# Moving four output stores behind a query transpose, and reordering batch 0's mean products

## The chip, the cores and the metric

The kernel runs on one core of one Trainium2 chip. The metric is the device time of one execution in microseconds (us). TensorE is called PE, VectorE DVE, ScalarE ACT, GpSimd POOL; SyncE (SP) issues transfers only. A row with a q (SPq, POOLq) is the issue of a transfer on that engine's queue.

## What is computed

Linear attention over 8 batches, 8 heads, 576 positions and 64 channels per head, followed by a feed-forward block over the 512 channels of all heads:

```
q_s = exp(q) / sum over channels        k_s = exp(k) / sum over positions
kv  = k_s^T v   (per head, 64 x 64)     x   = q_s kv   (576 x 512 per batch)
xn  = (x - mean(x)) / sqrt(var(x) + 1e-6) * g
out = x + relu(xn @ w1) @ w2            w1: 512 x 2048, w2: 2048 x 512
```

The maxima that the reference takes off before the exponentials cancel in the quotients. Inputs and output are float32; the products run in bfloat16.

## The kernel before

The 576 positions of a batch are cut into 512 main positions (4 tiles t of 128) and 64 left over. A chunk c from 0 to 7 is the main part of batch c; chunk 8 gathers the left-over positions of all batches. For each chunk the feed-forward products are a list of small steps, `mlp_steps(c)`. Beside it stands a list of side steps with hand-written positions, which prepare the next batches: loads, exponentials, transposes, kv products and x. `run(main, side)` merges the two lists by position, so the order on every engine is the one written by hand (`manual_schedule`); each engine takes its instructions strictly in that order and waits on semaphores where data is missing.

**What lies around the stores.** Chunk 0's outputs come from `y_out` (L512): DVE forms `ot` (L516), and POOL's queue stores it (L522), 256 KB each, four in all, one for each tile t. They come at the end of chunk 0's steps. Then `run` for c = 1 begins, with the side steps of `second_side` (L889): batch 2's queries are exponentiated (positions 3 and 9) and transposed by a transfer on SP's queue (`eq_T(2)`, position 14, L253). At 14.1 `load_batch(3, (2,), ...)` lets POOL copy four elements of the transposed queries eqT into batch 3's query buffer (L1114, a CAST in the profile), so that SP's load of batch 3's queries (L117) starts only when the transposes have landed. At 14.2 `load_v(3)` has POOL load batch 3's v (vt, vr; L144, L147). Behind SP's loads of q, k and the rest of k (ktr, L124) stand, on the same queue, the transposes of chunk 2's normalised x (`xn_T`, xnT). From xnT, POOL forms the differences tq (`sum_x`, L245) that chunk 2's first layer uses: `mm1_fast` (L751) computes it as products of sums and differences of blocks, with banks bx, bb and bc. The buffers `ot` are a ring of four; chunk 1's outputs (`y_quarter`, L607) write the same four again.

**What lies around the mean.** Batch 0 is the start of the kernel. There x is built transposed: `xt_mm(j)` multiplies the queries of tiles 0 and 1 with kv for block j of 128 channels. The mean over channels is a product as well: `mean0(i)` scales a constant matrix by a row sum of kv (DVE, L320), and `mean_mm(i, ns)` adds the i-th of four such products to target n: 0 is the mean alone (xm), 1 and 2 are blocks 2 and 3 of x. Blocks 0 and 1 get the mean added later on DVE (`xt_out(0)`, `xt_out(1)`, L356); blocks 2 and 3 have it in the bank already (L361 on DVE, L363 on ACT). Behind these PE has eight po products for x itself, then the transposes of query tile 2 (`eq_pT(0, 2)`, L932), which need ACT's exponential of the second half of batch 0's q.

Of the kernel before, what the change touches and what calls it, by code (L numbers as in the profile page):

```python
# [20 lines left out]
def kernel(  # L21
# [16 lines left out]
    nc = tc.nc  # L38

    B, H, S, D = q.shape  # L40
# [3 lines left out]
    T = 4  # L44
    SM = P * T
# [3 lines left out]
    NP = H // 2  # L49
# [51 lines left out]
    def main_src(x, b, h0, hn):  # L101
        return x[b, h0 : h0 + hn, 0:SM, :].rearrange("h (p t) d -> p h (t d)", t=T)
# [19 lines left out]
    def load_krem(eng, b):  # L122
        for half in range(2):
            eng.dma_start(  # L124
                raws[b][3][SR * half : SR * half + SR],
                k[b, 4 * half : 4 * half + 4, SM:S, :].transpose([1, 0, 2]),
            )
# [11 lines left out]
    def load_v(b):  # L139

        vts[b] = mlp.tile([P, H, T, D], BF16, tag="vt", name="vt", bufs=1)
        if b == 1:
            load_krem(nc.gpsimd, b)
        nc.gpsimd.dma_start(vts[b].rearrange("p h t d -> p h (t d)"), main_src(v, b, 0, H))  # L144
        for half in range(2):
            hs = slice(4 * half, 4 * half + 4)
            nc.gpsimd.dma_start(  # L147
                vr[SR * half : SR * half + SR, b % 2, hs, 0:D],
                v[b, hs, SM:S, :].transpose([1, 0, 2]),
            )  # L150
# [13 lines left out]
    eks, eqs, eqTs, xs, xnTs, rstds, tqs = {}, {}, {}, {}, {}, {}, {}  # L164
# [21 lines left out]
    def exp_q(b, j, hn=2):  # L186
        if j == 0:
            new_eq(b)
        hs = slice(2 * j, 2 * j + hn)
        nc.scalar.activation(  # L190
            eqs[b][0][:, :, hs, :].rearrange("p t h d -> p h t d"),
            raws[b][2][:, hs], AF.Exp,
        )
# [11 lines left out]
    def reduce_q(c, t, tn=1):  # L205
        ts = slice(t, t + tn)
        nc.vector.reduce_sum(eqs[c][1][:, ts], eqs[c][0][:, ts], axis=AX.X)  # L207
# [49 lines left out]
    def eq_T(c):  # L257
        dma_T(eqTs[c], eqs[c][0].rearrange("p t h d -> p (t h d)"), 0, T)
# [63 lines left out]
        )  # L322

    def mean_mm(i, ns):
        if i == 0 and 0 in ns:
            kvbox["m"] = mm_ps.tile([P, 2, 2, P], FP32, tag="m", name="xm")[:, 0]
            both = mm_ps.tile([P, 2, 2, P], FP32, tag="m", name="xt")
            kvbox["xt", 2], kvbox["xt", 3] = both[:, 0], both[:, 1]
        for n in ns:
            nc.tensor.matmul(  # L330
                (kvbox["m"], kvbox["xt", 2], kvbox["xt", 3])[n], mean_w[:, i],
                eqTs[0][:, 0:2, i, :], start=(i == 0 and n < 2), stop=(i == NP - 1),
                skip_group_check=True,
            )

    def xt_mm(j):

        if j < 2:
            kvbox["xt", j] = att_ps.tile([P, 2, 2, P], FP32, tag="a", name="xt")[:, 0]
        nc.tensor.matmul(  # L340
            kvbox["xt", j], kv_sb[:, 0, j, :], eqTs[0][:, 0:2, j, :],
            start=(j < 2), stop=(j < 2), skip_group_check=True,
        )

    def y_mul(j):
# [81 lines left out]
    def square_sum(c, t):  # L427
        x, _, _, mv = xs[c]
        nc.scalar.activation(  # L429
            scrap, x[:, t], AF.Square, bias=mv[:, t, 0:1], scale=-float(DM),  # L430
            accum_out=mv[:, t, 1:2],
        )
# [26 lines left out]
    def rstd_op(c):  # L459
        mv = xs[c][3]  # L460
        lnv = sml.tile([P, T], FP32, tag="lnv", name="lnv")
        rstds[c] = mlp.tile([P, T], FP32, tag="rstd", name="rstd")
        nc.scalar.activation(
            lnv, mv[:, :, 1], AF.Ln, bias=eps_ln, scale=1.0 / DM ** 3
        )
        nc.scalar.activation(rstds[c], lnv, AF.Exp, scale=-0.5)
# [24 lines left out]
    def mm1_part(c, m, t0, tn, ko):  # L491
# [13 lines left out]
        if m % 2 == 1 and at + tn == 2 and ko == KO1 - 1:  # L505
# [3 lines left out]
            else:  # L509
                nc.scalar.activation(dst, ph, AF.Relu)  # L510

    def y_out(c, t, pc, cols=slice(0, 512), eng=None):  # L512
        if cols.start == 0:
            hbox["ot"] = outp.tile([P, DM], FP32, tag="ot", name="ot")
        ot = hbox["ot"][:, cols]
        nc.vector.scalar_tensor_tensor(  # L516
            ot, in0=pc, scalar=rstds[c][:, t : t + 1], in1=xs[c][0][:, t, cols],
            op0=ALU.mult, op1=ALU.add,
        )
        eng = eng or nc.gpsimd  # L520
        if c < B:
            eng.dma_start(  # L522
                out[c, 0:SM, :].rearrange("(p t) n -> p t n", t=T)[:, t, cols], ot
            )
        else:
            for half in range(2):
                eng.dma_start(
                    out[2 * t + half, SM:S, cols], ot[64 * half : 64 * half + 64]
                )

    def mm2(c, t, ko):
        if ko == 0:
            hbox["pc"] = mm_ps.tile([P, DM], FP32, tag="m", name="pc")
        nc.tensor.matmul(
            hbox["pc"], hbox["h"][:, ko, t, :], w2_sb[:, ko, :],
            start=(ko == 0), stop=(ko == KO2 - 1),
        )
        if ko == KO2 - 1:
            y_out(c, t, hbox["pc"])
# [12 lines left out]
    def quarter_w2(i, g):  # L552

        ks = slice(4 * g, 4 * g + 4)
        rows = [w2_sb[:, 8 * g + odd : 8 * g + 8 : 2, :] for odd in range(2)]
        (b11, b12), (b21, b22) = [(r[:, :, 0:DH2], r[:, :, DH2:DM]) for r in rows]
        t1, t2, t3, t4 = [w2_q[:, n, ks, :] for n in range(4)]
        dst, x, y = ((t1, b12, b11), (t3, b22, b12), (t2, b22, t1), (t4, b21, t2))[i]
        nc.vector.tensor_sub(out=dst, in0=x, in1=y)
# [329 lines left out]
    def second_side():  # L889

        s = [(p, lambda i=i: quarter_w2(i, 1)) for i, p in enumerate((13, 16, 44, 46))]
        s += [(8, lambda: xn_pT(1, 2, nc.scalar)), (12, lambda: xn_pT(1, 3, nc.vector))]
        s += [(3, lambda: exp_q(2, 0, 4)), (9, lambda: exp_q(2, 2, 4)), (14, lambda: eq_T(2))]
        s += [(42, lambda: square_sum(1, 2)), (67, lambda: square_sum(1, 3)), (71, lambda: rstd_op(1))]
        s += [(14.1, lambda: load_batch(3, (2,), eqTs[2][0:1, T - 1, NP - 1, 0:4])), (31, lambda: load_batch(3, (0,)))]
        s += [(18 + 2 * j, lambda j=j: cast_v(2, j)) for j in range(2)]
        s += [(14.2, lambda: load_v(3))]
        s += [(93 + j, lambda j=j: cast_v(3, j)) for j in range(2)]
        s += [(15 + 3 * t, lambda t=t: reduce_q(2, t, 2)) for t in (0, 2)]
        s += [(36, lambda: recip_q(2))]  # L900
        s += [(18, lambda: exp_k(2, 0, 4)), (22, lambda: exp_k(2, 2, 4)), (26, lambda: prep_kvrem(2))]
        s += [(41, lambda: kv_all(2))]
        s += [(46, lambda: start_x(2))]
        for t, (p0, p1) in enumerate(((52, 54), (57, 59), (62, 65), (70, 74))):
            s += spread([lambda t=t, i=i: po_mm(2, t, i) for i in range(NP)], p0, p1)
            s += [(p1, lambda t=t: x_fast(2, t)), ((73, 82, 88, 94)[t], lambda t=t: square_sum(2, t))]
        s += [(60, lambda: xn_T(2, 0, 2)), (77, lambda: xn_T(2, 2, 2)), (100, lambda: rstd_op(2))]
        s += [(75, lambda: exp_q(3, 0, 4)), (79, lambda: exp_q(3, 2, 4)), (85, lambda: eq_T(3))]
        s += [(97, lambda: exp_k(3, 0, 4)), (108, lambda: exp_k(3, 2, 4)), (113, lambda: prep_kvrem(3))]
        s += [(p, lambda i=i: sum_w1(i, 1)) for i, p in ((2, 28), (3, 30))]  # L910
        s += spread([lambda i=i: sum_x(2, i) for i in range(4)], 95, 108)
        return s
# [39 lines left out]
    def xn_pT(c, t, eng):  # L952
        pe_T(xnTs[c], xs[c][2][:, t], t, eng, None if c else g_col)
# [7 lines left out]
    def first_batch():  # L961
# [94 lines left out]
        y_mul(0)  # L1056
        xt_mm(1)
        y_mul(1)
        for i in range(2):
            mean_mm(i, (0,))  # L1060
        for i in range(2):
            mean_mm(i, (1, 2))
        xt_mm(2)
        xt_mm(3)
        for i in (2, 3):
            mean_mm(i, (0,))
        for i in (2, 3):
            mean_mm(i, (1, 2))
        exp_qt(0, 2)
        exp_qt(0, 3)  # L1070
        xt_out(0)
# [1 line left out]
        for t in range(2):  # L1073
            pobox[0, t] = mm_ps.tile([P, DM], FP32, tag="m", name="po")
            for i in range(NP):
                nc.tensor.matmul(
                    pobox[0, t][:, i * P : i * P + P], eqTs[0][:, t, i, :], kv_sb[:, 0, i, :],
                    start=True, stop=True,
# [28 lines left out]
    def load_batch(b, parts=(2, 0), after=None):  # L1107

        alloc(b, parts)
        for which in parts:  # L1110
            if after is None:
                nc.vector.memset(raws[b][which][0:1, 0, 0, 0:1], 0.0)
            else:
                nc.gpsimd.tensor_copy(out=raws[b][which][0:1, 0, 0, 0:4], in_=after)  # L1114
        for which in parts:
            load_main(nc.sync, b, which, 0, H)
        if 0 in parts:
            load_krem(nc.sync, b)
# [102 lines left out]
```

## Time and profile before

| | |
|---|---|
| median of 3 runs | 265.62 us (264.61 to 266.18) |
| profiled execution | 265.17 us, of which the span of the profile is 263.0 us |
| granted clock of PE | 0.996 of full speed, mean |
| DMA | 45.00 MB, mean 171 GB/s |
| stores of the output on POOL's queue | 32 of 256 KB, median 5.9 us from issue to landing |
| transposes of the queries on SP's queue | 7, median 4.9 us from issue to landing |

How to read the lines shown: in a group or timeline row stand the start and the busy time in us (in the page's groups only the busy time), the engine, the line of the kernel, the operation, output and input, the shape, the count, and in square brackets how long the engine sat idle before it and what ended that. A row of the chain is start, duration and work; "DMA" in it is a transfer from issue to landing. A row of the table of windows gives, for each engine, its busy time in that stretch with the count of instructions, then the granted clock, the share of the 16 DMA engines' time that was busy, and GB/s.

### The profile page before, as it was taken

Reading aid. Unit: us, or ns where it says so; the run is one execution under the profiler, and the core shown is the slowest. Engines: PE = TensorE matmul, PEld = TensorE weight load, DVE = VectorE, ACT = ScalarE, POOL = GpSimd, SP = SyncE. Lnnn points to the kernel's source line nnn. Section 1 sums busy time; section 2 is a strip of 40 time slices with the busy share of each in tenths; the row PEclk is TensorE's granted clock in tenths of the full one; section 3 lists DMA queues with packets and bytes.
Section 4 is the critical chain, followed back from the end, with each engine's and each line's share of the span. In section 5 each row is a group of like instructions: output and inputs, shape, how many; then the busy total and the mean of one; then the engine's idle time right before and its main releaser. Section 6 shows DMA issues by size and latency. Waiting matters only on the chain.

```text
span 263.0 us, 6841 instructions
## 1 busy us (share of the span) xinstructions
PE 255.7 (97%) x2708; PEld 216.9 (82%) x2711; DVE 217.6 (83%) x482; ACT 180.5 (69%) x357; POOL 77.8 (30%) x129
## 2 busy tenths in 40 slices
PE   8989999999999999999999999999999999999993
PEld 6779755866888998899889988998899888888882
DVE  5767677988888897989798979997989889977873
ACT  4867571997966888688868886888688378447400
POOL 8652237203049007600760067007300300030000
PEclk9999999999999999999999999999999999999998
DMA  6999999987988975899589976997804620621014
GB/s 226 247 202 206 321 237 300 274 167 244 197 151 243 303 116 97 213 302 144 93 228 293 145 88 193 331 131 159 262 1 78 175 74 3 79 102 60 0 42 120
DMA packets 69895, 45.00 MB, mean 171 GB/s; under 512 B 41508, under 2 KB 66088, under 8 KB 69864
## 3 DMA queue, kind: packets, MB, share of 16 engines
q0 software_dynamic: 20368, 22.29, 38.9%
q1 hardware_dynamic: 48896, 21.76, 38.8%
q10 hardware_dynamic: 600, 0.53, 0.6%
q8 instruction: 21, 0.34, 0.5%
q14 instruction: 10, 0.08, 0.1%
HBM read 36.70 MB, written 9.44 MB: 175 GB/s over the span
## 4 chain that ended last, share of the span: by engine, by line
PE 87%; DMA 6%; POOL 2%; DVE 2%; ACT 1%; issue 1%; POOLq 0%
PE bx L748 18%; PE ba L596 18%; PE bb L748 9%; PE ph L499 8%; PE pc L545 5%; PE bc L748 5%; PE bb L596 5%; PE be L596 5%; PE bc L596 5%; DMA qt<-in_q_dram 4%; DMA xnT<-xn 3%; PE ph L484 3%; PE po L415 2%; PE pkv L379 2%; PE ptr L932 1%; DVE hs L576 1%
## 5 line engine op out<-in xcount | busy, mean ns | idle before, releaser
L596 PEld LDWEIGHTS <-hs 128*128 128x128 bf16 x512 | 49.6, 98 | 5.7
L748 PEld LDWEIGHTS <-w_q 128*128 128x128 bf16 x448 | 43.2, 98 | 5.5 <-issue 0.6
L596 PEld LDWEIGHTS <-hT 128*128 128x128 bf16 x392 | 37.3, 98 | 4.4
L245 POOL TENSOR_TENSOR tq<-xnT 128x256 bf16<-128x256 bf16 x20 | 12.9, 660 | 78.7 <-DMA xnT<-xn 64.3
L748 PEld LDWEIGHTS <-w1g 128*128 128x128 bf16 x336 | 32.2, 98 | 3.9
L596 PE MATMUL ba<-w_q,hs 128*128 128x256 bf16 x256 | 31.7, 273 | 0.0
L748 PE MATMUL bx<-tq,w_q 128*128 128x256 bf16 x224 | 29.0, 273 | 0.2 <-ACT s L776 0.2
L613 POOL DMA_DIRECT2D out_dram<-ot x28 | 15.3, 557 | 45.6 <-DVE ot L607 45.6
L429 ACT ACTIVATE scrap<-x,mv 128x512 bf16<-128x512 bf16 x36 | 26.0, 721 | 1.8 <-DVE x L445 1.4
L445 DVE SCALAR_TENSOR_TENSOR x<-po,rq 128x512 bf16<-128x512 f32 x34 | 23.3, 684 | 1.3 <-PE po L415 1.2
L772 ACT COPY bc<-bx 128x512 f32<-128x512 f32 x28 | 15.2, 596 | 13.0 <-PE bx L748 13.0
L779 DVE TENSOR_TENSOR bb<-bx,s 128x512 f32<-128x512 f32 x28 | 18.2, 694 | 6.9 <-ACT s L776 6.9
L790 ACT ACTIVATE hT<-bc 128x512 bf16<-128x512 f32 x28 | 15.3, 595 | 12.5 <-PE bc L748 12.5
L207 DVE TENSOR_REDUCE zq<-eq 128x16 f32<-128x1024 bf16 (+1 forms) x20 | 20.8, 1051 | 2.1 <-ACT eq L190 1.7
L576 DVE TENSOR_TENSOR hs<-hT 128x1024 bf16<-128x1024 bf16 x32 | 20.9, 674 | 0.9 <-ACT hT L790 0.5
L790 ACT ACTIVATE hT<-bb 128x512 bf16<-128x512 f32 x28 | 15.2, 595 | 8.4 <-PE bb L748 8.4
L782 DVE TENSOR_TENSOR hT<-bx,s 128x512 bf16<-128x512 f32 x28 | 18.0, 684 | 2.8 <-PE bx L748 2.8
L415 PE MATMUL po<-kv_sb,eqT 128*128 128x128 bf16 x120 | 20.2, 219 | 0.0
L621 ACT COPY s<-ba 128x512 f32<-128x512 f32 x15 | 8.7, 579 | 11.9 <-PE ba L596 7.3
L596 PE MATMUL ba<-w_sb,hT 128*128 128x256 bf16 x128 | 16.7, 273 | 0.0
L596 PE MATMUL bb<-w_q,hs 128*128 128x256 bf16 x128 | 16.5, 273 | 0.0
L190 ACT ACTIVATE eq<-qt 128x1024 bf16<-128x1024 f32 x14 | 14.6, 1056 | 1.9 <-DMA qt<-in_q_dram 1.9
(149 smaller groups left out, 542.9 us busy)
## 6 DMA issues: line engine op xcount, KB each, us to landing
out_dram<-ot POOLq DMA_DIRECT2D x32, 256.0 KB, 5.9
qt<-in_q_dram SPq DMA_DIRECT2D x5, 1024.0 KB, 6.5
kt<-in_k_dram SPq DMA_DIRECT2D x5, 1024.0 KB, 14.3
vt<-in_v_dram POOLq DMA_DIRECT2D x7, 512.0 KB, 14.4
qt<-in_q_dram POOLq DMA_DIRECT2D x2, 1024.0 KB, 13.0
kt<-in_k_dram POOLq DMA_DIRECT2D x2, 1024.0 KB, 14.8
kt<-in_k_dram SPq DMA_DIRECT2D x4, 288.0 KB, 4.7
w_raw<-in_moe_w_ch_dram POOLq DMA_DIRECT2D x4, 256.0 KB, 10.0
```

The costliest lines, as they stand in the source:

```text
L207: nc.vector.reduce_sum(eqs[c][1][:, ts], eqs[c][0][:, ts], axis=AX.X)
L415: nc.tensor.matmul(pobox["p"][:, i * P : i * P + P], eqTs[c][:, t, i, :], kv_sb[:, c, i, :], start=True, stop=True,)
L429: nc.scalar.activation(scrap, x[:, t], AF.Square, bias=mv[:, t, 0:1], scale=-float(DM), accum_out=mv[:, t, 1:2],)
L445: nc.vector.scalar_tensor_tensor(x[:, t].rearrange("p (h d) -> p h d", h=H), in0=pobox[c, t].rearrange("p (h d) -> p h d", h=H), scalar=1. ...
L499: nc.tensor.matmul(ph[:, m % 2, at : at + tn], (w1g if c else w1_sb)[:, ko, m * P : (m + 1) * P], xnTs[c][:, t0 : t0 + tn, ko, :], start=( ...
L576: nc.vector.tensor_tensor(out=dst, in0=x, in1=y, op=op)
L596: nc.tensor.matmul(dst, lhsT, rhs, start=first and (own or t == 0) and k == 0, stop=k == KH - 1, skip_group_check=True)
L613: nc.gpsimd.dma_start(out[c, 0:SM, :].rearrange("(p t) n -> p t n", t=T)[:, t], ybox[c, t])
L748: nc.tensor.matmul(dst[:, q], lhsT, rhs, start=first and q == 0 and ko == 0, stop=ko == 1, skip_group_check=True)
L779: nc.vector.tensor_tensor(out=at[g, "b"], in0=at[g, "x"], in1=at[g, "s"], op=ALU.add)
L782: nc.vector.tensor_tensor(out=h_out(g, 1, 1), in0=at[g, "x"], in1=at[g, "s"], op=ALU.add)
L790: nc.scalar.activation(h_out(g, odd, half), at[g, name], AF.Relu)
```

## The change

First, `y_out` no longer stores chunk 0's outputs but notes them in a list `late`; a new side step `store_late` at position 14.2 of chunk 1 issues the four stores, behind the CAST that waits for batch 2's transposed queries and ahead of `load_v(3)`, which is now at 14.3. Second, in batch 0 all four mean products of target 0 come first, then the eight of targets 1 and 2, and only then `xt_mm(2)` and `xt_mm(3)`, which now close the accumulation. In the built program the number of instructions on every engine is unchanged; the order differs on POOL (the four stores stand behind the CAST) and on PE (these products; and a wait for ACT's L363 moves from the transposes of query tile 3 to the ph product just ahead of them).

```diff
     def mean_mm(i, ns):
-        if i == 0 and 0 in ns:
+        if i == 0 and ns == (0,):
             ...
             nc.tensor.matmul(
                 (kvbox["m"], kvbox["xt", 2], kvbox["xt", 3])[n], mean_w[:, i],
-                eqTs[0][:, 0:2, i, :], start=(i == 0 and n < 2), stop=(i == NP - 1),
-                skip_group_check=True,
+                eqTs[0][:, 0:2, i, :], start=(i == 0 and n < 2),
+                stop=(i == NP - 1 and n == 0), skip_group_check=True,
             )
...
     def xt_mm(j):
             ...
-            start=(j < 2), stop=(j < 2), skip_group_check=True,
+            start=(j < 2), stop=True, skip_group_check=True,
...
+    late = []
+
     def y_out(c, t, pc, cols=slice(0, 512), eng=None):
...
-        if c < B:
+        if c == 0:
+            late.append((t, ot))
+        elif c < B:
             eng.dma_start(
                 out[c, 0:SM, :].rearrange("(p t) n -> p t n", t=T)[:, t, cols], ot
             )
...
+    def store_late():
+        for t, ot in late:
+            nc.gpsimd.dma_start(
+                out[0, 0:SM, :].rearrange("(p t) n -> p t n", t=T)[:, t, :], ot
+            )
...
-        s += [(14.2, lambda: load_v(3))]
+        s += [(14.2, store_late), (14.3, lambda: load_v(3))]
...
-        for i in range(2):
-            mean_mm(i, (0,))
-        for i in range(2):
-            mean_mm(i, (1, 2))
+        for ns in ((0,), (1, 2)):
+            for i in range(NP):
+                mean_mm(i, ns)
         xt_mm(2)
         xt_mm(3)
-        for i in (2, 3):
-            mean_mm(i, (0,))
-        for i in (2, 3):
-            mean_mm(i, (1, 2))
```

## The prediction

> **What bounds the kernel now.** I read the page first (busy times, chain), then the chain by stage, then the POOL and SP queues around the moved stores, the table of windows for the DMA, and the timeline of batch 0.
>
> ```profile
> PE 255.7 (97%) x2708; PEld 216.9 (82%) x2711; DVE 217.6 (83%) x482; ACT 180.5 (69%) x357; POOL 77.8 (30%) x129
> ...
> PE 87%; DMA 6%; POOL 2%; DVE 2%; ACT 1%; issue 1%; POOLq 0%
> ```
>
> PE is busy 255.7 of 263.0 us and carries 87% of the chain. An edit that adds no matmul can only fill or open the holes of PE. Two holes lie where the change works: one in batch 0, one at the start of chunk 2. The chain shows the second:
>
> ```profile
> 68.63 7.05 DMA xnT<-xn
> ...
> 76.17 1.30 POOL tq L245 x2
> ...
> 77.52 0.61 PE bb L748 x4
> ...
> 78.77 1.03 PE bx L748 x8
> ```
>
> The second transpose of chunk 2's x (xnT) is issued at 68.63 and lands at 75.68. POOL forms the first differences tq behind it, and PE's bb waits for them. Matmuls of 256 columns follow each other here at 0.109 us (16 in the 1.75 us of the chain's L748 pieces). So the eight bx from 76.42 allow bb at 77.29; it starts at 77.52, a hole of 0.23. Eight bb allow the next bx at 78.39; it starts at 78.77, a hole of 0.38 (the second pair of tq ends at 78.71, and ACT's s at 78.74). Together 0.6 us: what this place can give back. It has no slack the other way: whatever makes that xnT later makes tq and PE later by as much.
>
> Why the xnT takes 7.05 us is seen upstream, in POOL's queue and then SP's:
>
> ```profile
> 47.96 1.22 POOL L522 DMA_DIRECT2D out_dram<-ot  x2 [2.06 <-DVE ot L516]
> 51.27 0.54 POOL L522 DMA_DIRECT2D out_dram<-ot  x1 [2.09 <-DVE ot L516]
> 53.32 0.54 POOL L522 DMA_DIRECT2D out_dram<-ot  x1 [1.51 <-DMA vt<-in_v_dram]
> 59.10 0.18 POOL L1114 CAST qt<-eqT 1x4 f32<-1x4 bf16 x1 [5.25 <-DMA eqT<-eq]
> 60.37 0.91 POOL L144 DMA_DIRECT2D vt<-in_v_dram  x1 [1.09 <-DVE w_q L559]
> ```
>
> ```profile
> 52.50 3.33 SPq L253 DMA_TRANSPOSE eqT<-eq  x1
> 59.30 0.40 SPq L117 DMA_DIRECT2D qt<-in_q_dram  x1
> 59.88 0.45 SPq L117 DMA_DIRECT2D kt<-in_k_dram  x1
> 60.42 2.36 SPq L124 DMA_DIRECT2D ktr<-in_k_dram  x2
> 64.32 8.77 SPq L253 DMA_TRANSPOSE xnT<-xn  x2
> ```
>
> Batch 2's query transposes (eqT) go out at 52.50 and land 6.5 us later, at 59.0. The CAST on POOL waits for them, SP's loads of batch 3 (q, then k and its rest) wait for the CAST, and the xnT transposes stand behind those loads on SP's queue.
>
> ```profile
> 58.00:60.00 2.00, 2.00 (x34) 1.08 (x27) 1.49 (x4) 1.78 (x5) 0.18 (x1) 1.00 0.00 0
> 60.00:62.00 2.00, 2.00 (x14) 1.01 (x12) 1.36 (x3) 1.20 (x3) 1.63 (x3) 1.00 0.61 166
> ```
>
> The last columns are the DMA share and GB/s: nothing moves from 58 to 60, then comes a burst (328 to 347 GB/s from 62 to 66) up to the end of the xnT.
>
> **Part 1, the stores.** Removed ahead of the CAST: four issues of 256 KB. Added behind it, in front of vt's load on POOL: the same four, 0.55 us each in these rows, 2.2 us. No instruction of PE, DVE or ACT changes place in the built program. Four terms:
>
> *(a) eqT lands earlier.* Its last competitor is the fourth store, issued at 53.32 and landed 5.5 us later (58.8). Other eqT transposes, all without a store between issue and landing, took 4.3 us (issued at 97.9), 4.9 (150.3), 5.0 (73.2) and 6.2 (124.1). So eqT lands between 56.8 and 58.7: earlier by 0.3 to 2.2. I take 4.6 us, 57.1, earlier by 1.9: near the short end, because the 5.0 still had an xnT in front of it and this eqT has nothing. The Trainium skill (DMA: Bandwidth & Descriptors, Queues, rings and completion order) says that a completion increment lands only after every earlier write of that DMA engine, across its queues. The trace agrees in that store and eqT land 0.2 us apart; by that rule alone the whole 2.2 would come.
>
> *(b) The loads move with it.* q's issue goes from 59.30 to 57.4; k's needs the kt memset of DVE (57.41), which still comes in time.
>
> *(c) The stores now share the burst.* Two later chunks have q, k, v and four stores together. Chunk 2: q issued at 78.83, first store at 81.17, so the stores join late; the rest of k landed 14.3 us after q's issue (13.2 after its own, 79.94). Chunk 3: first store at 105.04, q at 105.48; the rest of k landed 17.2 us after q's issue (108.27 plus 14.4). Now, without stores, it is 13.7 us (62.12 plus 10.9, against 59.30). So the stores add 0.6 to 3.5 us. In the changed kernel CAST frees stores and q at the same moment, so it is nearer to chunk 3. But its DMA has room at first: 166 GB/s from 60 to 62 against 337 (the window 62 to 66), which is about 1.0 us of transfers. I take 2.3, some 60% of the way from 0.6 to 3.5. The xnT stands behind the rest of k on SP's queue and is late by as much as that.
>
> *(d) vt's load* goes behind four issues: CAST's end at 57.3 plus 2.2 gives 59.5, against 60.37 now. It lands 12.8 us after issue now (73.16), and 11.0 (chunk 2) or 14.5 (chunk 3) beside stores: 70.5 to 74.0. Who waits: DVE's cast_v at 73.16 and behind it the four L607 pairs up to 77.66; the second half of PE's bb, at about 77.96, needs the last of these. Slack 0.3 us; a vt at 74.0 would cost 0.5, in the same stretch as (c), so the larger of the two counts, not the sum.
>
> The stores' own landing costs nothing. Their buffers are next written by L607 at 73.84. Issued up to 59.5 and landing within the 9.1 us of chunk 3's slowest, they are free at 68.6. If that cover of 5.2 us went, L607 would stall and PE's bb behind it. POOL has no other work up to tq at 76.17.
>
> Sum for part 1: +2.3 − 1.9 = +0.4 us at the xnT, and as much for PE. Bounds: −0.6 (all gain, the holes closed) to 3.5 − 0.3 = +3.2.
>
> **Part 2, the mean.** No instruction is added; PE takes all four mean products for xm, then the eight for blocks 2 and 3, then the two xt_mm. The fourth xm product now needs DVE's last scaling (11.86 plus 0.49, so 12.35) at 12.23: PE waits some 0.15 us. xm is complete at 12.7, not 13.2, and DVE's L356 can start at 12.8 instead of 13.29; blocks 2 and 3 end 0.15 later on PE (13.6 against 13.44). All of it disappears in one hole:
>
> ```profile
> 14.90 0.40 PE L932 MATMUL ptr<-ident,eq 128*128 128x128 bf16 x4 [0.85 <-ACT eq L198]
> ```
>
> PE's next work, the transposes of query tile 2, waits for ACT's exponential of q's second half, whose DMA lands at 14.20 in the chain (4.88 plus 9.32). ACT's xt_out(3) stays behind those exponentials (L363, 15.28 plus 0.45). One wait moves: in the built program the ph product of 16.16 now waits for this L363, as the transposes behind it did before; at 15.73 it is done, 0.4 us ahead. So part 2 costs 0 while that landing holds; without this cover it could give 0.5 (L356's lead) or take 0.15. I take 0.
>
> **Sum.** The profiled execution took 265.17 us (span 263.0, 2.2 around it): 265.6 after. The median of the runs is 0.45 above it: 265.6 + 0.4 = 266.0.
>
> **Rivals.** *Earlier transposes win* (0.26): eqT lands at 56.8 and the stores join the burst late, as in chunk 2. Then the rest of k lands 14.3 us after 57.1, at 71.4 instead of 73.0, xnT 1.6 earlier, and the holes of 0.6 close: median 265.0. For: the idle DMA from 58 to 60. Against: the stores do not start 2.3 us after q, as there.
>
> *The burst is the bound* (0.22): this is the slower side. The stores' 1.05 MB at 337 GB/s (mean of 62 to 66) are 3.1 us of DMA that used to run in a stretch where nobody waited, from 48 to 58, and now run ahead of a landing with no slack. With eqT earlier by only 1.4 (the mean of the four landings, 5.1) xnT lands 1.7 later: PE stalls 1.7, median 267.3. It decides when xnT lands after 77.0. For: chunk 3's row; the DMA share is 1.0 or more in every two microseconds from 62 to 72 save one of 0.98. Against: the free time at the start. The Trainium skill (DMA: Bandwidth & Descriptors, Rules for kernel authors) says as much: issuing from another engine brings no bandwidth, since all run on the same 16 DMA engines and interleave. By its ceiling of 435 GB/s the stores would be 2.4 us, an estimate, and the stall 1.0.
>
> *It moves nothing* (0.12): eqT was late for reasons of its own (6.2 us at 124.1 without a store), the loads keep their time, and the stores fit into the free start of the burst: 265.6.
>
> **How the numbers follow.** Forecast 0.40, at 266.0. A measurement of this kernel can tell about 0.5%, 1.3 us, from no change. Faster by more: only where the hole at 77 is larger in unprofiled runs than the 0.6 seen, 0.05 out of the 0.26. Slower by more: the burst case with 0.22, and 0.03 of the forecast's upper tail. The rest, 0.70, is within. The range runs from the case of earlier transposes less 0.2 for the spread of the runs (264.8) to the burst case plus 0.3 (267.6); under 264.8 and over 267.6 I leave about 0.1 each.
>
> **What would show it.** Right: CAST at about 57.1, q's load at 57.4, four stores behind CAST, vt issued at 59.5; the second xnT at about 76.1 with tq at 76.6; holes of PE at 77 to 79 of about 1.0 instead of 0.6; L356 at 12.8 and ptr still at 14.90. Wrong: CAST still near 59 (term a), xnT before 75.1 or after 77.0 (term c), DVE waiting for vt or for a store's landing (term d), or ptr off 14.90 (part 2).

## The result, and the profile after

The kernel after the change takes 266.2 us (median of 22 runs, 265.3 to 268.7); the kernel before, beside it, 265.0 us (22 runs, 263.58 to 267.58). The ratio is 1.005, 95% interval 1.0028 to 1.0072: slower by 1.2 us between the medians, 1.3 by the ratio. The profiled execution after took 266.8 us with a span of 264.5; the one before 265.17 with 263.0.

From the page of the kernel after, the busy row of PE with its neighbours, and the chain by engine:

```profile
PE 255.8 (97%) x2708; PEld 217.0 (82%) x2711; DVE 217.5 (82%) x482; ACT 180.5 (68%) x357; POOL 78.0 (29%) x129
...
PE 87%; DMA 6%; DVE 3%; POOL 2%; issue 1%; ACT 0%; POOLq 0%
```

PE's work is the same 255.8 us, so the 1.5 us of span are holes of PE. The tables of windows say where. First the kernel before, then the one after (columns: length, PE, PEld, DVE, ACT, POOL busy with counts, granted clock, DMA share, GB/s):

```profile
0.00:20.00 20.00, 17.62 (x282) 13.70 (x283) 12.72 (x43) 13.05 (x30) 14.11 (x27) 1.00 1.05 225
70.00:80.00 10.00, 9.73 (x101) 8.26 (x100) 7.76 (x18) 7.14 (x15) 3.83 (x7) 1.00 1.01 131
80.00:90.00 10.00, 10.00 (x125) 9.01 (x118) 8.93 (x18) 7.09 (x14) 5.56 (x9) 1.00 0.99 316
```

```profile
0.00:20.00 20.00, 18.27 (x290) 14.33 (x291) 13.07 (x44) 12.85 (x30) 14.11 (x27) 1.00 1.05 225
70.00:80.00 10.00, 7.82 (x70) 6.67 (x69) 6.53 (x16) 5.74 (x13) 2.24 (x4) 1.00 1.20 156
80.00:90.00 10.00, 9.78 (x123) 8.48 (x121) 7.90 (x15) 7.03 (x14) 7.16 (x12) 1.00 0.87 278
```

PE gains 0.65 us of work in the first 20 us, loses 1.91 from 70 to 80 and 0.22 from 80 to 90: together 1.48, the whole difference of the spans. The loss lies at the start of chunk 2, as forecast. The earlier work at the start buys nothing, since PE waits at chunk 2 in both profiles; it only makes the hole there longer. The chain there:

```profile
70.90 6.37 DMA xnT<-xn
...
77.76 1.31 POOL tq L245 x2
...
79.11 0.61 PE bb L758 x4
...
80.37 1.03 PE bx L758 x8
```

The second xnT is issued 2.3 us later than before (70.90 against 68.63) and lands at 77.27 against 75.68, 1.6 us later; tq and PE's bb follow by the same 1.6. Why it is issued later is seen in the last normalised x of chunk 2 (xn) and in how long the two issues hold SP's queue. From the chain and the rows of xnT, before and then after (the three numbers are the shortest, median and longest issue in ns):

```profile
68.23 0.35 DVE xn L437
...
L253 SPq DMA_TRANSPOSE xnT<-xn x2: 4213/4338/4462, 64.3 to 68.6; - x2
```

```profile
67.54 0.35 DVE xn L437
...
L253 SPq DMA_TRANSPOSE xnT<-xn x2: 4002/5545/7088, 63.7 to 70.9; - x2
```

Before, the second transpose goes out at 68.63, as soon as its xn is there (68.58). After the change its xn is there at 67.89, but the first transpose, issued at 63.72, holds the queue for 7.09 us instead of 4.21, and the second goes out only at 70.90.

The timeline of POOL and then of SP's queue show the moved steps:

```profile
56.67 0.18 POOL L1119 CAST qt<-eqT 1x4 f32<-1x4 bf16 x1 [11.46 <-DMA eqT<-eq]
57.22 2.18 POOL L537 DMA_DIRECT2D out_dram<-ot  x4 [0.37 <-DVE rq L883]
60.04 0.91 POOL L144 DMA_DIRECT2D vt<-in_v_dram  x1 [0.64 <-DVE w_q L569]
```

```profile
51.81 3.08 SPq L253 DMA_TRANSPOSE eqT<-eq  x1
56.87 0.40 SPq L117 DMA_DIRECT2D qt<-in_q_dram  x1
57.44 0.45 SPq L117 DMA_DIRECT2D kt<-in_k_dram  x1
57.99 5.63 SPq L124 DMA_DIRECT2D ktr<-in_k_dram  x2
63.72 11.18 SPq L253 DMA_TRANSPOSE xnT<-xn  x2
```

The CAST comes at 56.67 instead of 59.10, q's load at 56.87 instead of 59.30: the transposes do land earlier. What becomes of these 2.4 us is in the lists of DMA issues in the window from 50 to 63 us (KB each, us from issue to landing), before and after:

```profile
kt<-in_k_dram SPq DMA_DIRECT2D x1, 1024.0 KB, 11.4
...
vt<-in_v_dram POOLq DMA_DIRECT2D x1, 512.0 KB, 12.8
ktr<-in_k_dram SPq DMA_DIRECT2D x2, 64.0 KB, 10.9
```

```profile
out_dram<-ot POOLq DMA_DIRECT2D x4, 256.0 KB, 8.3
kt<-in_k_dram SPq DMA_DIRECT2D x1, 1024.0 KB, 15.6
vt<-in_v_dram POOLq DMA_DIRECT2D x1, 512.0 KB, 14.3
ktr<-in_k_dram SPq DMA_DIRECT2D x2, 64.0 KB, 14.8
```

k takes 4.2 us longer, its rest 3.9, v 1.5. A load that started 2.4 us earlier ends later. There is also a wait that the prediction did not have. The timeline of ACT, and then of PE, after the change:

```profile
73.05 1.06 ACT L171 ACTIVATE ek<-kt 128x1024 bf16<-128x1024 f32 x1 [1.77 <-DMA kt<-in_k_dram]
...
74.44 0.57 ACT L631 COPY s<-ba 128x512 f32<-128x512 f32 x1
```

```profile
72.24 1.91 PE L606 MATMUL be<-w_sb,hs 128*128 128x256 bf16 x16
75.05 1.91 PE L606 MATMUL ba<-w_q,hT 128*128 128x256 bf16 x16 [0.91 <-ACT s L631]
76.80 1.04 PE L758 MATMUL bx<-xnT,w1g 128*128 128x256 bf16 x8
79.11 1.03 PE L758 MATMUL bb<-tq,w_q 128*128 128x256 bf16 x8 [1.28 <-POOL tq L245]
```

ACT's exponential of batch 3's k waits for k's landing; ACT's copy of ba (L631) stands behind it; PE's next ba waits for that copy. With 0.109 us for each matmul, be allows ba at 73.99 (hole 1.06), bx allows bb at 77.67 (hole 1.44), and bb allows the next bx at 79.98 (hole 0.39, ended at 80.37): 2.9 us of holes where the profile before had 0.6.

### The profile page after: what moved, and what is told of

Read it like the earlier page. It is cut to its first block, busy times and chain, and to the rows that moved or that the text cites. A ratio compares the mean times of both kernels' runs of the same rounds, so it can differ in the third digit from the quotient of the medians.

```text
span 264.5 us, 6840 instructions
## 1 busy us (share of the span) xinstructions
PE 255.8 (97%) x2708; PEld 217.0 (82%) x2711; DVE 217.5 (82%) x482; ACT 180.5 (68%) x357; POOL 78.0 (29%) x129
## 4 chain that ended last, share of the span: by engine, by line
PE 87%; DMA 6%; DVE 3%; POOL 2%; issue 1%; ACT 0%; POOLq 0%
PE bx L758 18%; PE ba L606 18%; PE bb L758 9%; PE ph L499 8%; PE pc L555 5%; PE bc L758 5%; PE bb L606 5%; PE be L606 5%; PE bc L606 5%; DMA w_raw<-in_moe_w_ch_dram 3%; PE ph L484 3%; DMA xnT<-xn 2%; PE po L415 2%; PE pkv L379 2%; DVE hs L586 2%; PE ptr L942 1%
## 5 line engine op out<-in xcount | busy, mean ns | idle before, releaser
L245 POOL TENSOR_TENSOR tq<-xnT 128x256 bf16<-128x256 bf16 x20 | 12.9, 660 | 81.3 <-DMA xnT<-xn 66.8
L800 ACT ACTIVATE hT<-bc 128x512 bf16<-128x512 f32 x28 | 15.3, 594 | 12.4 <-PE bc L758 12.4
L631 ACT COPY s<-ba 128x512 f32<-128x512 f32 x15 | 8.7, 579 | 11.9 <-PE ba L606 7.3
L786 ACT COPY s<-bb 128x512 f32<-128x512 f32 x28 | 15.5, 622 | 1.3 <-PE bb L758 1.3
## 6 DMA issues: line engine op xcount, KB each, us to landing
qt<-in_q_dram POOLq DMA_DIRECT2D x2, 1024.0 KB, 12.8
```

The lines of the kernel that those rows point to most:

```text
L786: nc.scalar.copy(at[g, "s"], at[g, "b"])
L800: nc.scalar.activation(h_out(g, odd, half), at[g, name], AF.Relu)
```

## The experiments

The ratios compare with runs of the kernel before that were taken beside each group of runs (medians 265.42 us for e1 to e4, 265.20 for e5 to e7, 265.53 for e8); they are estimates with an interval and differ a little from the quotients of the medians (for e3 that quotient is 0.9956). "Stores" are chunk 0's four. The third column is the range of the runs.

| run | median us | range | ratio to before (95%) |
|---|---|---|---|
| the change | 266.2 | 265.3–268.7 | 1.005 (1.0028–1.0072) |
| e1: stores late, mean as before | 266.48 | 265.73–267.0 | 1.0029 (1.0002–1.0056) |
| e2: mean alone | 265.79 | 264.12–268.92 | 1.0008 (0.9977–1.0040) |
| e3: change, stores behind v's load | 264.26 | 263.72–264.98 | 0.9939 (0.9915–0.9963) |
| e4: change, stores left out | 263.93 | 263.35–264.75 | 0.9924 (0.9898–0.9949) |
| e5: change, only the fourth store late | 264.36 | 263.58–265.71 | 0.9969 (0.9947–0.9991) |
| e6: change, exponential of k later | 266.55 | 265.23–267.75 | 1.0038 (1.0013–1.0063) |
| e7: change, only the fourth store late, behind v | 264.21 | 263.87–264.74 | 0.9954 (0.9937–0.9971) |
| e8: as e3, mean as before | 264.25 | 263.57–265.1 | 0.9950 (0.9928–0.9973) |
| e9: before again, one run | 263.98 | | |
| e10: mean alone again, one run | 266.83 | | |

### The two parts, each alone (e1, e2)

e1 keeps the late stores and puts the mean back; e2 keeps the mean and puts the stores back.

```diff
 # e1, against the kernel after
...
-        for ns in ((0,), (1, 2)):
-            for i in range(NP):
-                mean_mm(i, ns)
+        for i in range(2):
+            mean_mm(i, (0,))
+        for i in range(2):
+            mean_mm(i, (1, 2))
         xt_mm(2)
         xt_mm(3)
+        for i in (2, 3):
+            mean_mm(i, (0,))
+        for i in (2, 3):
+            mean_mm(i, (1, 2))
 # e2, against the kernel after
-        if c == 0:
-            late.append((t, ot))
-        elif c < B:
+        if c < B:
...
-        s += [(14.2, store_late), (14.3, lambda: load_v(3))]
+        s += [(14.2, lambda: load_v(3))]
```

> The late stores alone, with batch 0's products in the old order. Theory A (the stores fill the burst that ends in chunk 2's xnT): as slow as the whole change, 1.0 to 1.4 us over the kernel before; the second xnT lands some 20 us after batch 3's query load is issued, against 16.4 before. Theory B (the new order of the mean products costs part of it, 0.15 us of waiting on PE or more): 0.3 us or more faster than the whole change.

> The new order of batch 0's products alone, with the stores in their old place. Theory A: the same as before within 0.3 us, since PE's transposes of query tile 2 and the first w1 block's landing hide it; DVE's L356 starts 0.4 to 0.5 us earlier. Theory B: 0.3 us or more slower than before.

The stores alone are slower (1.0029), the mean alone makes no difference that these runs can tell. In e1's trace k takes 14.8 us, the rest of k 13.9, and tq starts at 77.64, as after the change. So the loss belongs to the stores; for the mean, e2's interval leaves 0.6 us of gain to 1.1 of loss open, and e8 below narrows it.

### Is it the stores' place, or their bytes? (e3, e4)

e3 exchanges two steps, so that the stores are issued behind v's load; every byte still moves. e4 leaves the stores out.

```diff
-        s += [(14.2, store_late), (14.3, lambda: load_v(3))]
+        s += [(14.2, lambda: load_v(3)), (14.3, store_late)]   # e3
+        s += [(14.3, lambda: load_v(3))]                       # e4
```

> The whole change, but the four stores are issued on POOL behind batch 3's v load instead of ahead of it. Theory A, told more closely (each DMA engine takes packets from the two queues in turn, and what counts is which of POOL's packets are ahead when k's are sent): v's packets take the place that the stores had, k lands earlier by 1 to 3 us than with the change, and the second xnT lands 1 to 2 us earlier: 0.3 us slower to 0.4 us faster than before. Rival C (bytes in the burst count, whatever their order): the same as the change, 1.0 to 1.4 us over before.

> The whole change, but chunk 0's four stores are left out altogether, so the main part of batch 0 is not written. Theory A: the query transposes land early as with the change (4.6 to 5.0 us after issue), the burst has no stores, the second xnT lands about 16.4 us after batch 3's query load, and the 0.6 us of holes at chunk 2's start close: 0.3 to 0.8 us faster than before. Rival D (the loads of batch 3 are slower by themselves when they start 2 us earlier, because of what else runs then): 0.5 us or more slower than before.

e3 is the version that beats both kernels: 0.9939. POOL's timeline, the DMA list of the same window, and the chain of e3:

```profile
57.14 0.91 POOL L144 DMA_DIRECT2D vt<-in_v_dram  x1 [0.34 <-DVE rq L883]
...
59.44 2.19 POOL L537 DMA_DIRECT2D out_dram<-ot  x4
```

```profile
kt<-in_k_dram SPq DMA_DIRECT2D x1, 1024.0 KB, 11.7
out_dram<-ot POOLq DMA_DIRECT2D x4, 256.0 KB, 12.7
vt<-in_v_dram POOLq DMA_DIRECT2D x1, 512.0 KB, 12.6
ktr<-in_k_dram SPq DMA_DIRECT2D x2, 64.0 KB, 10.3
```

```profile
67.84 7.74 DMA xnT<-xn
...
75.72 1.31 POOL tq L245 x2
```

With the stores 2.2 us later on POOL's queue, k takes 11.7 us instead of 15.6 and its rest 10.3 instead of 14.8; now the stores take 12.7 instead of 8.3, and nobody waits for them. The second xnT goes out at 67.84, 3.1 us before the changed kernel's, again as soon as its xn is there (67.81): the first one's issue took only 3.23 us. k comes 3.9 us earlier where 1 to 3 were expected, and both e3 and e4 are faster than theory A had them (at most 0.4 and 0.8 us). Rivals C and D fall.

The bytes are not free, though. Without any store (e4) k takes 11.1, the second xnT lands 4.6 us after its issue instead of 7.74, and the first tq starts at 73.45 instead of 75.72. In the time little of this is left, 0.33 us, no more than the intervals leave open: in e3 PE could take bb at 76.53 and waits for tq until 77.07, and in e4 it does not wait for tq at all. So of the first tq's lateness after the change (77.76) the place of the stores explains 2.0 us against e3, and their bytes 2.3 more, most of them in the slack that PE has there (one profile each; e8 below, with the stores in the same place as e3, has 76.17). What e3 does not separate: its stores stand behind v's load and are also 2.2 us later than q and k; which of the two counts is open. How the DMA engines share their time among the two queues was not measured either.

### One store at a time (e5, e7)

Of the four stores only the fourth is issued in the stretch in which the transposes of batch 2's queries run (52.0 to 53.3 in the profiles of before). e5 moves it alone, to where the change put all four; e7 moves it alone, behind v's load.

```diff
-        if c == 0:
+        if c == 0 and t == T - 1:
             late.append((t, ot))
...
-        s += [(14.2, store_late), (14.3, lambda: load_v(3))]
+        s += [(14.2, lambda: load_v(3)), (14.3, store_late)]   # e7 only
```

> The whole change, but the first three stores go out where they used to and only the fourth waits behind the CAST, ahead of v's load. Theory A (each store ahead of v costs its share; the fourth alone was in eqT's way): eqT lands 4.6 to 5.0 us after issue as with all four moved, and the burst carries a quarter of the stores, so k lands 11.5 to 13 us after its issue instead of 15.6: 0.4 to 1.2 us faster than before. Rival E (eqT is freed only when all four stores are gone): eqT over 6 us, no gain over before.

> The first three stores where they used to be, the fourth behind batch 3's v load; the mean products in the new order. Theory A: eqT as early as with the change, k and v land as without stores (11.1 to 11.7 and 12.6 to 12.9 us after issue), and only one store is left in front of or beside the xnT: between the variant with all four behind v (1.2 us faster than before) and the one without them (1.5 us faster). If the four stores behind v cost nothing at all, it is level with that variant within 0.3 us.

With the fourth store away eqT lands 5.0 us (e5) and 5.5 us (e7) after its issue, nearly as early as with all four away. k was not as expected in either: 13.7 us in e5, where 11.5 to 13 were expected, and 13.0 in e7 (v 13.4), where nothing stands ahead of v and 11.1 to 11.7 were expected (v 12.6 to 12.9). So k's own time does not count the stores ahead of v in proportion. The first tq keeps the order: 74.94 in e7, 76.68 in e5 with one store ahead of v, 77.76 with four. The windows of e7, and then of e5:

```profile
70.00:80.00 10.00, 10.00 (x125) 8.73 (x124) 8.52 (x20) 6.41 (x15) 5.06 (x9) 1.00 0.76 148
```

```profile
70.00:80.00 10.00, 9.42 (x86) 8.15 (x84) 7.54 (x18) 7.45 (x17) 3.32 (x6) 1.00 1.06 141
```

e7 has no hole at chunk 2 at all, e5 one of 0.6. Both beat the kernel before. That e7 beats e3 is not shown: 264.21 and 264.26.

### Does the new wait of ACT cost anything? (e6)

e6 puts the exponential of k's first half behind the copy L631 on ACT, so that the copy no longer waits for k.

```diff
-        s += [(97, lambda: exp_k(3, 0, 4)), (108, lambda: exp_k(3, 2, 4)), (113, lambda: prep_kvrem(3))]
+        s += [(108, lambda: exp_k(3, 0, 4)), (108, lambda: exp_k(3, 2, 4)), (113, lambda: prep_kvrem(3))]
```

> The whole change, but ACT's first exponential of batch 3's k is put behind its copy of s3, so the copy no longer stands behind the wait for k's landing. Theory A (xnT's landing sets chunk 2's start, and the hole of 1.1 us that the copy makes earlier lies in its shadow): the hole at ba goes, the hole at bb grows by as much, and the time is that of the change within 0.4 us, about 1 us over before. Rival F (the copy's wait is what the change costs): 0.8 to 1.1 us faster than the change, level with before.

In e6 the copy L631 runs at 72.47, behind ba itself. The timeline of PE:

```profile
74.02 1.91 PE L606 MATMUL ba<-w_q,hT 128*128 128x256 bf16 x16
76.13 1.03 PE L758 MATMUL bx<-xnT,w1g 128*128 128x256 bf16 x8 [0.21 <-DMA xnT<-xn]
78.79 1.75 PE L758 MATMUL bb<-tq,w_q 128*128 128x256 bf16 x8 [1.63 <-POOL tq L245]
```

The hole ahead of ba is gone, and the wait for tq has grown from 1.28 to 1.63, with one of 0.21 ahead of bx. The time is no better (1.0038, and its interval excludes the level of before, which rival F named). The wait of ACT was real, but it lay in the shadow of the xnT's landing. (In this profile PE's granted clock fell to 0.88 from 80 to 90 us, so its span of 265.5 is not read.)

### What the old order of the stores does (e8, e9, e10)

e3, e4, e5 and e7 gain 0.8 to 1.5 us, more than the holes of 0.6 in the first profile allow. Either the mean's order brings 0.7 at the start (theory G), or the holes of before are larger in other executions. e8 is e3 with the mean put back (the diff of e1); e9 is the kernel before, e10 the kernel of e2, unchanged, each for a second profile.

> Chunk 0's stores behind batch 3's v load, as in the third run, but the mean in the order of before. Theory A (the mean's order brings nothing, whatever the stores do): the time equals that of the third run, ratio to before 0.992 to 0.996. Theory G (the mean's order brings the 0.7 us by which the products ptr started earlier in four of six profiles with the new order (14.05 to 14.24 against 14.90), and the run with the mean's order alone lost it again in chunk 2's burst): 0.7 us slower than the third run, ratio 0.9965 to 0.999, and ptr starts at 14.8 to 14.9.

> The kernel before, unchanged, for a second profile of the old orders: nothing is changed in it. Theory A says that the two holes of chunk 2's transpose vary from execution to execution: in this profile PE busy between 70 and 80 us may be anywhere from 8.0 (as with the mean's order alone) to 9.7 (as in the first profile). Theory G says that the first profile is typical: ptr starts at 14.8 to 15.0 behind q's second half, and PE is busy 9.5 us or more between 70 and 80 us.

> The mean's order alone once more, for a second profile. Theory A: PE's busy time between 70 and 80 us can be anywhere from 8.0 to 9.7, and ptr anywhere from 14.1 to 15.1, with no tie to the order. Theory G: ptr starts at 14.0 to 14.3 again, and PE is busy 8.0 to 8.3 us between 70 and 80 us, since an earlier start meets a transpose that lands no earlier.

e8 takes 264.25, e3 264.26: the 0.7 us of theory G are not there, though runs that spread over 1.3 and 1.5 us cannot exclude a difference of some 0.5. And the early start appears with the old order as well: ptr at 13.82 in e8 and at 14.26 in e9. Theory G falls. Four profiles have the stores in their old place, and they differ at chunk 2; the window of e9, with the same kernel as the first profile and no hole (10.00, more than the 9.7 that theory A expected at most):

```profile
70.00:80.00 10.00, 10.00 (x126) 8.82 (x124) 8.61 (x20) 6.46 (x15) 5.49 (x9) 1.00 0.80 125
```

| stores in the old place | eqT, issue to landing | first tq | PE busy 70 to 80 | this execution |
|---|---|---|---|---|
| e9 (before) | 6.1 us | 74.51 | 10.00 | 263.98 us |
| first profile of before | 6.5 us | 76.17 | 9.73 | 265.17 us |
| e2 (mean alone) | 8.0 us | 77.33 | 7.99 | 266.37 us |
| e10 (mean alone) | 9.4 us | 77.79 | 8.66 | 266.83 us |

The longer eqT takes, the later tq and the longer the execution. (In e10 PE already waits 1.0 us for eqT itself, at 61.04, so that its hole at chunk 2 is shorter than e2's.) In the first profile, e2 and e10 the fourth store, which took 5.5, 7.3 and 8.7 us, landed 0.2 us ahead of eqT; in e9 it took 3.7 and landed 2.3 us ahead. Why the store's time varies so much is not shown.

How tq sets the time is seen in what follows it: from the start of the first tq to the end of the span it is 186.7 to 186.9 us in six profiles in which PE waits for tq (before, after, e1, e2, e5, e10) and 186.5 in e3 and e8. Among the six, ptr starts anywhere from 14.01 to 14.99: an earlier start does not shorten what follows tq, which is why the 0.65 us of the first 20 us bought nothing.

In the five profiles with all four stores behind the CAST (after, e1, e3, e6, e8) eqT took 4.8 to 5.0 us, in e4 4.6. So the old place costs a varying 1.1 to 4.8 us at eqT, and the first profile showed it near its small end. That four profiles fall in this order is a correlation; e4, e5 and e7, which take the fourth store out of that stretch and gain, are the test of it.

## Why the prediction was right, and where it was not

The time of 266.2 lies in the range, 0.2 from the forecast, and the direction, a little slower, is right. But that the time is met so closely is luck: the difference was forecast as 0.4 us and is 1.2 to 1.3, and the forecast stood on a median of three runs (265.62) that was 0.6 above that of the 22 runs taken beside the change. Three of the prediction's own signs of being wrong came: the second xnT landed after 77.0 (term c), DVE waited for vt (term d), and ptr was off 14.90 (part 2). Step by step:

- **(a) eqT lands earlier: right.** Forecast 4.6 us from issue to landing, measured 4.8. The CAST came at 56.67 (forecast 57.1), 2.4 us earlier than before; 0.7 of it is that eqT was itself issued earlier (51.81 against 52.50), so 1.7 to 1.8 come from the stores, against the 1.9 of the forecast. By the rule of the Trainium skill (DMA: Bandwidth & Descriptors, Queues, rings and completion order) the whole 2.2 would have come; the trace stays below that. What one profile could not show is that the time of the old place varies from 6.1 to 9.4 us.
- **(b) the loads move with it: right.** q at 56.87 instead of the forecast 57.4, k at 57.44.
- **(c) the stores share the burst: the term that was mis-sized.** Forecast +2.3 from a range of 0.6 to 3.5. From q's issue to the landing of the rest of k it is now 17.9 us (60.0 plus 14.8, less 56.87) instead of 13.7: +4.2, outside the range. The error was the discount for the DMA's free start from 60 to 62. Chunk 3's row, where the first store stood 0.4 us ahead of q (17.2 us), was the nearest and should have been taken whole. Taken whole, 3.5 less the 1.9 of (a), it gives the 1.6 by which the xnT landed later. −2.4 + 4.2 gives +1.8 for the rest of k. That the xnT is late by as much as the rest of k held for this pair, but not by standing behind it: the loads' issues ended at 63.62 and the first xnT went out at 63.72, 0.16 behind its xn. What was late is the second, behind the long issue of the first, a step that the prediction does not have. In e3 the rest of k lands by 70.6 and the xnT 5 us after it. Why the first issue takes 7.09 us is not shown; without a store ahead of v and with an early eqT (e3, e4, e7, e8) it takes 2.5 to 3.8.
- **(d) v behind four stores: the landing came just outside the bounds.** vt was issued at 60.04 and landed at 74.3 (forecast 70.5 to 74.0): DVE waited for it, its busy time from 72 to 74 is 0. That the larger of (c) and (d) counts held: bb waited for tq, not for v.
- **The stores' own landing: right**, no one waited for it (8.3 us from issue, against a cover up to 73.84).
- **Not foreseen:** ACT's exponential of k as a waiter, with PE's ba behind it, a hole of 1.06 us. e6 shows that it costs nothing while the xnT is late.
- **Part 2, the mean: right at 0, though not for its whole reason.** L356 starts at 12.79 (forecast 12.8), and PE's weight load waits 0.16 us for the last scaling (forecast 0.15). But ptr came at 14.05, not at 14.90: the landing of q's second half, which was to hide all, is earlier in most profiles, under both orders. The ph behind it then waits for a weight, 14.67. e8 against e3 shows no gain or loss of it above some 0.5 us.
- **"What this place can give back" is 0.6: wrong.** e3, e7 and e8 gain 1.0 to 1.3 us. The profiled execution was an ordinary one in time (265.17 against medians of 265.0 to 265.5), but its hole was one of many sizes: with the stores in their old place the first tq ran from 74.51 to 77.79 in four profiles. With all four or the fourth alone behind v, or left out (e3, e8; e7; e4), it ran from 73.45 to 76.17.

Of the rivals, "The burst is the bound" named its own point, an xnT that lands after 77.0, and it landed at 77.27: the size lies between the forecast and this rival. But its reason, that the stores' 3.1 us of DMA must be paid ahead of that landing, is only a part of it: in e3 the same bytes also land ahead of the second xnT (some 73 against 75.58), and the kernel gains. By e4 the bytes are 2.3 us of that landing (73.3), the place 1.7 more (77.27). "Earlier transposes win" is what e3 and e7 do, by 1.2 and 1.0 us. The Trainium skill's ceiling of 435 GB/s (DMA: Bandwidth & Descriptors, Specifications) gave an estimated stall of 1.0; the xnT came 1.6 later in the trace, and e3 shows that the stores' place, which that estimate leaves out, is worth 1.9 us of time (266.2 against 264.26), where leaving the bytes out is worth 0.33 more (e4).

## What to carry to other kernels

When stores that nobody waits for are moved to let a wanted transfer land earlier, put them behind every load that somebody waits for, and look at the loads on the other queues as well: here 2.2 us later on the same queue turned a loss of 1.2 us into a gain of 1.2. Size shared bandwidth by the row whose order of issue is the same as the new one, and give no discount for a start that looks free. One profile of a stretch where a transfer competes is one draw: the spread of the runs (4 us before, 1.3 in e3) says how far the holes in it can be trusted.

## What was not expected of the hardware

- Four stores of 256 KB ahead of v's load lengthened k's load, on another queue, to between 14.8 and 15.6 us (e1, e6, after), from 9.5 to 11.4 with the stores in their old place (e9, e10, before, e2); behind v's load they left it at 11.7 and 12.4 (e3, e8).
- One 256 KB store issued within 1 us of a transpose was enough that this transpose took 6.1 to 9.4 us from issue to landing (four profiles); without it, 4.6 to 5.5 (e1, e3 to e8, after).
- Transposes hold SP's queue: the two of chunk 2's xnT take 11.18 us of issue in the changed kernel and 8.77 before. The first alone takes 2.5 us (e4) to 7.09 (after), and a long one delays the second even when the second's data are there: by 3.0 us after the change.
- The landing of q's second half, issued at 4.88, moves from one execution to the next: ptr behind it started at 13.82 to 15.13 across the profiles, without a tie to the order of the mean.
